# An mLSTM cell with a mixture-of-depths layer on one core: output gates loaded and outputs made some steps later, two batches' expert layers moved from step 8 to step 9

## The chip, the core and the metric

The kernel runs on one NeuronCore of a Trainium2 chip. The core has five engines that run beside each other, each with its own instruction queue in program order: TensorE (PE, matrix products and transposes into PSUM), VectorE (DVE), ScalarE (ACT), GpSimd (POOL) and SyncE (SP, which here only issues loads and the last store). Sixteen DMA engines move data between HBM and the on-chip memory; SP and POOL issue to them. The metric is device time in microseconds (us), the median over several executions. All data are float32.

## What is computed

There are 4 batches, 8 heads, 768 positions and a head width of 40. The recurrence over positions, then the expert layer over the rows of one batch:

```python
for t in range(S):
    m_new = np.maximum(f_gate[:, :, t] + m, i_gate[:, :, t])
    f_stab = np.exp(f_gate[:, :, t] + m - m_new)
    i_stab = np.exp(i_gate[:, :, t] - m_new)
    m = m_new
    C = f_stab[..., None, None] * C + i_stab[..., None, None] * np.einsum('bhd,bhe->bhde', vt, kt)
    n = f_stab[..., None] * n + i_stab[..., None] * kt
    h_tilde = np.einsum('bhde,bhe->bhd', C, qt)
    denom = np.maximum(np.abs(np.einsum('bhd,bhd->bh', n, qt)[:, :, None]), 1.0)
    o = 1.0 / (1.0 + np.exp(-o_gate[:, :, t]))
    y[:, :, t] = o * h_tilde / denom
# x[b, s] = the 8 heads of y side by side: 320 numbers
scores = np.einsum('bsd,d->bs', x, w_gate)
for b in range(B):
    top_idx = the 128 rows of x[b] with the highest scores
    ye = np.maximum(x[b, top_idx] @ w1, 0.0) @ w2          # 320 -> 1024 -> 320
    out[b] = x[b];  out[b, top_idx] += sigmoid(scores[b, top_idx])[:, None] * ye
```

## The kernel before

The sequence is cut into 12 steps n = 0 to 11 of 256 positions, three for each batch (batch b = n // 3). A step handles all 8 heads. The order of all work is written out by hand: every engine does its instructions in the order of the program text, and waits only for the data it needs and for buffers to come free.

**A step on TensorE** (lines 675 to 743): `scores(n)` multiplies k and q of the step; `turn(n + 1, "kT")` transposes the next step's k; `update(n + 1)` forms the next step's additions to the state C in the PSUM buffer pU, of which there is one; `read(n)` applies the states to q, `turn(n + 1, "qT")` transposes the next q, and `attend(n)` applies the masked scores to the weighted v. The second argument of turn is a number of `fill` products with no use of their own, which only keep TensorE going.

**The other engines in a step.** DVE: `masked(n)` applies the causal mask, `states(n + 1)` adds pU to the running states, `divide(n)` makes y. `router(i)` on DVE forms the scores of the rows of step i. ACT: copies out of PSUM (kT, qT), `widen`, and `sigmoid(n)`, which makes so from the output gates o. POOL: `weigh(n + 2)` weights v, `output(n)` makes x = y * so and `store(n)` sends it to the output. There are four buffers each of k, q, v, o and y, and three of so.

**The expert layer of a batch** needs the scores of its three steps. `spread(b, ...)` puts them side by side with TensorE transposes and an ACT copy; `ranks(b)` counts for each row how many scores are higher, half of it by DVE compares and half by ACT signs; `select(b)` makes a 0/1 matrix of the ranks; `numbers(b, ...)` turns that into row numbers (a small product on TensorE, then index arithmetic on DVE); `fetch(b)` gathers the 128 rows from the output with an indirect DMA issued by POOL; `fetched(b)` transposes them; `layer1`, `layer2` and `weighed` compute; `add(b)` is an indirect DMA from POOL that adds the result onto the output rows. `layers(n)`, lines 628 to 673, takes the place of the rest of step 8: it holds the layers of batches 0 and 1 and the selection of batch 2, and makes the outputs of steps 6, 7 and 8. Batch 2's layers run in step 11 and the tail, batch 3's in the tail.

**Loads.** Every load is issued by SP. `load(n)` is v, k and q of a step (320 KB each), `load_o(n)` its output gates (320 KB). Lines 100 to 107 issue the first ones, and the table `queue` (line 624) says in which step's program text the others stand. SP runs through that list in order and holds at an entry whose buffer is not yet free. Pieces of a load of k, v and o are rows of 40 floats.

## Time and profile before

| | us |
|---|---|
| median of 3 runs | 163.75 |
| lowest, highest | 161.92, 165.38 |
| the profiled execution, device time | 163.37 |
| its span, first to last instruction | 161.3 |

The granted clock of TensorE is 0.989 over the span. Time between the span and the device time, 2.07 us, lies around the instructions.

| Queue, kind | packets | MB | share of 16 engines |
|---|---|---|---|
| q1, hardware (loads by SP) | 89920 | 18.75 | 65.1% |
| q0, software (stores, fetches and adds by POOL) | 1728 | 4.92 | 11.0% |

How to read the rows that follow in the prediction. A row of the timeline is: start in us, duration in us, engine, line of the program, operation, output <- input, shape, count, and in brackets the idle time before it and what ended it. A row of the stages is: stretch in us, its length, then the busy time and the number of instructions of each engine, the granted clock of TensorE (1.00 is full speed), the share of the DMA engines and the GB/s that they moved. PEld is TensorE's loading of weights, which runs beside its products. An SPq row is SP issuing a DMA, not the transfer itself.

### The profile page before, as it was taken

The numbers are of one execution on the slowest core, as the hardware profiler recorded it, in microseconds if no ns is written. First come the engines' busy times: TensorE is split into PE (matmuls) and PEld (weight loads), VectorE is DVE, ScalarE is ACT, GpSimd is POOL, SyncE is SP. The second block draws the span as 40 slices with busy tenths as digits, with TensorE's granted clock in tenths as the row PEclk, the third lists the DMA queues.
The fourth block names the chain that finished last, engine by engine and source line by source line (L and its number), as shares of the span: only waits on it lengthen the run. The fifth ranks groups of instructions, "written<-read, shape, count | busy, mean of one in ns | idle before, by whom it ended". The sixth has DMA issues, their size and how long they took to land.

```text
span 161.3 us, 6676 instructions
## 1 busy us (share of the span) xinstructions
PE 144.5 (90%) x2864; PEld 125.4 (78%) x2864; DVE 95.2 (59%) x251; ACT 89.0 (55%) x179; POOL 84.5 (52%) x114
## 2 busy tenths in 40 slices
PE   7989899998998998899989989799999999999900
PEld 7779789997987987799878779579888897898500
DVE  6478384656769957594596542197776959411000
ACT  1667396566598747425475675874648669213000
POOL 7137278988575492892004969847480924212020
PEclk9999999999999999999999999999999999999995
DMA  4999899999979989999989999999513210330110
GB/s 88 198 163 196 137 169 205 188 186 205 194 169 227 187 161 208 175 262 296 157 240 232 206 266 172 216 190 184 100 45 87 46 39 4 81 41 0 53 51 2
DMA packets 91880, 24.31 MB, mean 151 GB/s; under 512 B 88097, under 2 KB 90466, under 8 KB 91842
## 3 DMA queue, kind: packets, MB, share of 16 engines
q1 hardware_dynamic: 89920, 18.75, 65.1%
q0 software_dynamic: 1728, 4.92, 11.0%
q8 instruction: 24, 0.39, 1.1%
q10 hardware_dynamic: 194, 0.13, 0.3%
q14 instruction: 14, 0.11, 0.2%
HBM read 19.20 MB, written 4.59 MB: 147 GB/s over the span
## 4 chain that ended last, share of the span: by engine, by line
PE 63%; DMA 14%; ACT 7%; issue 5%; DVE 5%; ACTq 1%; POOL 1%; DVEq 0%; POOLq 0%
PE pt L232 10%; DMA k<-in_k_dram 9%; PE pU L267 9%; PE py L576 8%; PE pH L332 7%; PE pH L322 6%; PE pU L560 6%; PE pS L300 4%; PE ph L560 2%; DMA i_sb<-in_i_gate_dram 2%; PE pU L564 2%; DMA xe<-out_dram,idx 2%; PE pX L498 2%; ACT sgn L423 1%; PE pt L221 1%
## 5 line engine op out<-in xcount | busy, mean ns | idle before, releaser
L244 POOL TENSOR_TENSOR wv<-v,cols 64x656 f32<-64x656 f32 x23 | 30.1, 1312 | 25.0 <-DMA v<-in_v_dram 14.1
L354 POOL TENSOR_TENSOR x<-y,so 128x320 f32<-128x320 f32 x24 | 21.1, 896 | 10.9 <-DVE y L346 4.2
L236 ACT COPY qT<-pt 128x512 f32<-128x512 f32 x24 | 13.8, 635 | 17.2 <-PE pt L232 17.2
L250 ACT ACTIVATE so<-o 64x320 f32<-64x320 f32 x48 | 22.4, 467 | 0.9
L234 ACT COPY kT<-pt 128x512 f32<-128x512 f32 x24 | 13.3, 587 | 15.0 <-PE pt L232 15.0
L369 DVE CUSTOM_DVE_ANT_0 scr<-x,wg 128x320 f32<-128x320 f32 x22 | 13.8, 628 | 8.1 <-POOL x L354 6.5
L576 PE MATMUL py<-w,hT 128*128 128x320 f32 x64 | 18.2, 437 | 0.3 <-ACT qT L236 0.3
L279 DVE TENSOR_TENSOR C<-pU,C 128x164 f32<-128x164 f32 x40 | 13.1, 327 | 7.0 <-PE pU L267 5.9
L267 PE MATMUL pU<-wv,k 128*64 128x82 f32 x384 | 16.5, 237 | 0.7 <-issue 0.7
L267 PEld LDWEIGHTS pU<-wv,k 128*64 128x64 f32 x384 | 14.5, 137 | 2.8 <-issue 2.2
L332 PE MATMUL pH<-wv,P 128*64 128x82 f32 x384 | 16.3, 237 | 0.0
L576 PEld LDWEIGHTS py<-w,hT 128*128 128x128 f32 x64 | 11.8, 190 | 5.1 <-ACT qT L236 0.5
L332 PEld LDWEIGHTS pH<-wv,P 128*64 128x64 f32 x384 | 14.4, 136 | 1.8 <-issue 1.0
L232 PE MATMUL pt<-ident,k 128*128 128x128 f32 x96 | 13.7, 279 | 2.3 <-DMA k<-in_k_dram 2.1
L361 POOL DMA_DIRECT2D out_dram<-x x22 | 13.9, 635 | 3.3 <-POOL x L354 3.3
L418 DVE TENSOR_SCALAR_CACHE_REDUCE cmp<-sb,x 128x768 f32<-128x768 f32 (+2 forms) x14 | 12.0, 857 | 6.0 <-ACT sb L412 5.7
L300 PE MATMUL pS<-qT,kT 40*64 40x64 f32 x768 | 14.8, 221 | 0.8 <-issue 0.5
L306 DVE TENSOR_TENSOR P<-pS,mask 128x1024 f32<-128x1024 f32 x12 | 14.6, 1214 | 0.6 <-PE pS L300 0.6
L523 POOL DMA_INDIRECT xe<-out_dram,idx x4 | 4.3, 1086 | 19.9 <-DVE den L341 13.8
L322 PE MATMUL pH<-C,qT 40*64 40x41 f32 x704 | 14.0, 229 | 0.8 <-issue 0.6
L300 PEld LDWEIGHTS pS<-qT,kT 40*64 40x64 f32 x768 | 12.8, 134 | 2.3 <-issue 0.7
L232 PE MATMUL pt<-ident,qw 128*128 128x128 f32 x96 | 13.1, 279 | 1.4 <-ACT qw L216 1.4
(141 smaller groups left out, 229.6 us busy)
## 6 DMA issues: line engine op xcount, KB each, us to landing
k<-in_k_dram SPq DMA_DIRECT2D x24, 160.0 KB, 5.0
q<-in_q_dram SPq DMA_DIRECT2D x12, 320.0 KB, 5.4
v<-in_v_dram SPq DMA_DIRECT2D x24, 160.0 KB, 4.8
o<-in_o_gate_dram SPq DMA_DIRECT2D x24, 160.0 KB, 5.0
out_dram<-x POOLq DMA_DIRECT2D x22, 160.0 KB, 4.4
w<-in_moe_w_dram SPq DMA_DIRECT2D x2, 640.0 KB, 5.8
w<-in_moe_w_dram SPq DMA_DIRECT2D x2, 512.0 KB, 6.0
out_dram<-x SPq DMA_DIRECT2D x2, 160.0 KB, 2.6
```

Source lines behind the costliest of these rows:

```text
L232: PE.transpose(pt[:, p, :], src[:, c, 2 * p:2 * p + 2, :].rearrange("s j d -> s (j d)"), ident)
L236: ACT.copy(out=T.rearrange("e p (u t) -> e t p u", t=2)[:, c], in_=pt)
L244: (DVE if n == 0 and r else POOL).tensor_tensor(out=wv_t[n % 3][o, :, :, r], in0=v_t[n % NB][o], op=OP.mult, in1=cols[s][o, 0:2, b * H:b * ...
L250: ACT.activation(out=so_t[n % 3][64 * c:64 * c + 64, r], in_=o_t[n % NO][64 * r:64 * r + 64, c], func=AF.Sigmoid)
L267: PE.matmul(pU[64 * j:64 * j + 64, c, p], k_t[n % NB][:, c, 2 * p + j, :], wv_t[n % 3][:, c, 2 * p + j], start=True, stop=True)
L300: PE.matmul(pS[o, j, c, p, :], kT[e, p, t], qT[e, p, t], start=True, stop=True)
L306: DVE.tensor_tensor(out=P.rearrange(flat), in0=pending[n].pop("pS").rearrange(flat), op=OP.mult, in1=mask.unsqueeze(1).to_broadcast([128, ...
L322: PE.matmul(g["pH"][64 * c:64 * c + 64, NP * j + p, r], g["qT"][e, p, t], state[n, 2 * c + r][e, p, :], start=(c, j) not in g["begun"], st ...
L332: PE.matmul(g["pH"][64 * c:64 * c + 64, NP * j + p], g["P"][:, j, c, p, :], wv_t[n % 3][:, c, 2 * p + j], start=(c, j) not in g["begun"], ...
L354: POOL.tensor_tensor(out=x.rearrange(order, j=2, d=D), in0=pending[n]["y"][:, r].rearrange("s (j p) d -> s j p d", j=2), in1=o.rearrange(o ...
L361: (POOL if n < N - 1 else SP).dma_start(out=out[b, a:a + 128, :].rearrange("(r t) d -> t r d", t=64), in_=x_t[b % 2][64 * c:64 * c + 64, 2 ...
L576: PE.matmul(d["py"], hT_t[:, f, half(b)], w2[:, f, :], start=(f == 0), stop=(f == NF - 1))
```

## The change

The loads of the output gates move back in SP's list, so that k, v and q of later steps stand ahead of them: o(0) behind load 2, o(1) behind load 3, and so on; loads 7, 8 and 9 move to earlier steps' text, the first-layer weights behind load 9. The outputs of steps 1 to 5 are made later, by the table `made` (step 7 makes 4 and 5), their scores by the table `scored`. Step 10 makes 10. `layers` now runs in step 9 and makes the outputs of 6, 7, 8 and 9. The spread of batch 0 moves from step 3 to step 4, its ranks, selection and numbers from step 4 to step 5. The spread of batch 1 moves from step 7 into `layers`, behind `read`, and into the buffer pU. `numbers(2)` and `fetch(2)` move from step 9 to step 10, and `add(1)` moves from the end of `layers` to behind `fetch(2)`, ahead of `output(10)`. The fills of step 2 go from 6 to 4 and those of step 5 from 4 to 2.

```diff
     wg = const.tile([128, DM], FP, name="wg")
+    load(2)
     load_o(0)
-    load(2)
-    load_o(1)
...
-        if pool is None:
+        if pool is ps_u:
+            pB = ps_u.tile([128, 2, 512], FP, name="pU")
+        elif pool is None:
...
-    queue = {0: (load, 3, load_o, 2), 1: (load, 4, load_o, 3, load, 5, load_o, 4), 2: (load, 6, load_o, 5),
-             4: (load, 7, load, 8, weights1, None, load_o, 6), 5: (load_o, 7, weights2, None, load_o, 8), 6: (load, 9),
-             7: (load, 10), 9: (load_o, 9, load_o, 10, load, 11, load_o, 11)}
+    queue = {0: (load, 3, load_o, 1), 1: (load, 4, load_o, 2, load, 5), 2: (load, 6, load_o, 3), 3: (load, 7),
+             4: (load, 8, load_o, 4, load_o, 5), 5: (load, 9, weights1, None, load_o, 6),
+             6: (load_o, 7, weights2, None), 8: (load_o, 8, load_o, 9, load, 10), 10: (load_o, 10, load, 11, load_o, 11)}
+    made = {0: (0,), 2: (1,), 3: (2,), 5: (3,), 7: (4, 5), 10: (10,)}
+    scored = {1: (0,), 3: (1,), 4: (2,), 6: (3,), 8: (4, 5), 10: (9,)}

     def layers(n):
         fetched(0)
         read(n)
+        dep[1] = {"sb": spread(1, 0, 2 * NS, ps_u)}
         ranks(1)
         select(1)
         attend(n)
         layer1(0, 0)
         numbers(1, ps_t.tile([128, 3], FP, name="pi", tag="t"))
         fetch(1)
-        sigmoid(n - 2)
+        sigmoid(6)
...
         turn(n + 1, "qT")
         dep[2] = {"sb": spread_copy(pB, 2 * NS)}
+        sigmoid(9)
+        output(9)
+        store(9)
         ranks(2)
         layer2(1)
         weighed(1)
         select(2)
         weigh(n + 2)
         update(n + 1)
         states(n + 1)
-        add(1)
...
-        if n == 8:
+        if n == 9:
             layers(n)
             continue
...
-        if n == 4:
+        if n == 5:
             ranks(0)
             select(0)
         if more:
-            turn(n + 1, "kT", (0, 2, 6, 2, 2, 4)[n] if n < 6 else 0)
+            turn(n + 1, "kT", (0, 2, 4, 2, 2, 2)[n] if n < 6 else 0)
             widen(n + 1)
         if 0 < n and more:
             update(n + 1)
-            if n != 9:
+            if n != 10:
                 states(n + 1)
-            if n not in (3, 6, 7, 9):
-                router(n - 1)
+            for i in scored.get(n, ()):
+                router(i)
...
         read(n)
-        if n == 9:
+        if n == 10:
             numbers(2, ps_s.tile([128, 2, 512], FP, name="pi", tag="s")[:, 0, 0:3])
             states(n + 1)
-        if n + 2 < N and n != 7:
+            fetch(2)
+            add(1)
+        if n < 8:
             weigh(n + 2)
...
-            if n in (3, 7):
-                dep[n // 4] = {"sb": spread(n // 4, 0, 2 * NS)}
-            if n not in (6, 7):
-                sigmoid(n)
+            if n == 4:
+                dep[0] = {"sb": spread(0, 0, 2 * NS)}
+            for i in made.get(n, ()):
+                sigmoid(i)
...
-        if n == 4:
+        if n == 5:
             numbers(0, spare(n + 1)[:, 1, 0:3])
-        if n == 9:
-            fetch(2)
-        if more and n not in (6, 7):
-            output(n)
-            store(n)
+        for i in made.get(n, ()):
+            output(i)
+            store(i)
```

More of the change, by code (lines that the diff above doesn't have):

```diff
@@ L637, in layers @@
         fetch(1)
-        sigmoid(n - 2)
-        output(n - 2)
-        store(n - 2)
+        sigmoid(6)
+        output(6)
+        store(6)
         layer1(0, 4)
@@ L643, in layers @@
         valued(0)
-        sigmoid(n - 1)
-        output(n - 1)
-        store(n - 1)
+        sigmoid(7)
+        output(7)
+        store(7)
         layer2(0)
-        router(n - 2)
-        router(n - 1)
+        router(6)
+        router(7)
         fetched(1)
         weighed(0)
-        sigmoid(n)
-        output(n)
-        store(n)
+        sigmoid(8)
+        output(8)
+        store(8)
         valued(1)
         layer1(1, 0)
-        router(n)
+        router(8)
         layer1(1, 4)
@@ L688, in _fast @@
             states(0)
-        if n in (3, 6, 11):
+        if n == 11:
             router(n - 1)
-        if n == 4:
+        if n == 5:
             ranks(0)
@@ L698, in _fast @@
             update(n + 1)
-            if n != 9:
+            if n != 10:
                 states(n + 1)
-            if n not in (3, 6, 7, 9):
-                router(n - 1)
+            for i in scored.get(n, ()):
+                router(i)
         if not more:
@@ L719, in _fast @@
             turn(n + 1, "qT")
-            if n in (3, 7):
-                dep[n // 4] = {"sb": spread(n // 4, 0, 2 * NS)}
-            if n not in (6, 7):
-                sigmoid(n)
+            if n == 4:
+                dep[0] = {"sb": spread(0, 0, 2 * NS)}
+            for i in made.get(n, ()):
+                sigmoid(i)
         else:
@@ L731, in _fast @@
         divide(n)
-        if n == 4:
+        if n == 5:
             numbers(0, spare(n + 1)[:, 1, 0:3])
-        if n == 9:
-            fetch(2)
-        if more and n not in (6, 7):
-            output(n)
-            store(n)
+        for i in made.get(n, ()):
+            output(i)
+            store(i)
         if n == 0:
```

## The prediction

> **What bounds the kernel now.** I read the page first, then the stages (one row a step: a step starts where TensorE starts its scores), then single rows.
>
> ```profile
> PE 144.5 (90%) x2864; PEld 125.4 (78%) x2864; DVE 95.2 (59%) x251; ACT 89.0 (55%) x179; POOL 84.5 (52%) x114
> DMA  4999899999979989999989999999513210330110
> PE 63%; DMA 14%; ACT 7%; issue 5%; DVE 5%; ACTq 1%; POOL 1%; DVEq 0%; POOLq 0%
> ```
> ```profile
> core 0: us, PE busy (x) PEld busy (x) DVE busy (x) ACT busy (x) POOL busy (x), PEclk, DMA share, GB/s
> 20.96:28.71 7.75, 7.59 (x214) 6.81 (x213) 4.54 (x12) 6.05 (x12) 6.20 (x18) 1.00 0.93 189
> ...
> 62.70:70.80 8.10, 7.00 (x194) 6.11 (x192) 6.02 (x14) 4.37 (x8) 6.84 (x8) 1.00 0.93 180
> 70.80:78.24 7.44, 7.44 (x217) 6.78 (x214) 3.63 (x9) 3.54 (x6) 2.38 (x2) 1.00 1.07 288
> 78.24:108.84 30.60, 28.41 (x358) 23.18 (x355) 18.53 (x45) 20.24 (x44) 17.22 (x18) 1.00 1.02 209
> 108.84:115.76 6.92, 6.92 (x201) 6.28 (x199) 5.16 (x16) 3.30 (x7) 4.09 (x3) 1.00 1.11 167
> ...
> 123.16:161.30 38.14, 29.42 (x347) 24.92 (x344) 15.09 (x44) 13.62 (x36) 10.34 (x11) 0.95 0.15 34
> ```
> TensorE carries the chain (63%), yet until about slice 28 the DMA engines are as full. The rows are steps 1, 6, 7, 8 (with the layers), 9 and 11 with the tail. Step 7 is TensorE without a gap (7.44 of 7.44); step 6 lost 1.1 us. What else TensorE does in a step:
>
> ```profile
> 29.80 1.60 PE L221 MATMUL pt<-hot 128*128 128x128 f32 x12
> 65.58 0.63 PE L232 MATMUL pt<-ident,k 128*128 128x128 f32 x4 [0.44 <-DMA k<-in_k_dram]
> 76.20 0.82 PE L405 MATMUL pB<-ident,x 128*128 128x128 f32 x6
> 76.95 1.36 PE L332 MATMUL pH<-wv,P 128*64 128x82 f32 x32
> ...
> 85.86 0.31 PE L517 MATMUL pi<-place,sel 128*128 128x3 bf16 x6
> ```
> A spread takes 76.95 - 76.20 = 0.75, so a bare step is 7.44 - 0.75 = 6.69; a fill is 1.60/6 = 0.27; numbers() 0.3. Steps 1 to 7 hold seven bare steps, 16 fills, two spreads and one numbers: 46.8 + 4.3 + 1.5 + 0.3 = 52.9. They took 78.24 - 20.96 = 57.3. So 4.4 us were lost there, in the stage where the queue of loads sets the pace (the wait for k in the row at 65.58 is one such place). That is what the change can win, with four fills.
>
> **The loading stage after the change.** SP's queue runs in program order, so the place of a tile in it, not the step, decides when it comes.
>
> ```profile
> 22.23 1.72 SPq L65 DMA_DIRECT2D v<-in_v_dram  x2
> ...
> 58.88 3.47 SPq L65 DMA_DIRECT2D k<-in_k_dram  x2
> ...
> 63.17 2.77 SPq L65 DMA_DIRECT2D v<-in_v_dram  x2
> 66.47 1.34 SPq L65 DMA_DIRECT2D k<-in_k_dram  x2
> ```
> From v3 (22.23) to v8 (63.17) the queue issued 19 tiles of 320 KB: 40.9/19 = 2.15 us each, the stores beside them counted in. k7's issue ended at 62.35 and TensorE went on with it at 65.58: landing takes 3.2 us more. After the change o stands behind k, v and q: k4 and k5 have one o fewer ahead of them, k6 to k8 two. Up to k9 there are now 29 tiles of k, v, q and six of o; up to k8 before, 26 and six, issued by 67.81. So k9 is three tiles later: 67.8 + 6.5 = 74.3, less one or two stores that are put off (stores 4 and 5 now follow step 7; an estimate of at most 2.15 each): 71 to 73, landed 74.2 to 76.2. Without any loss step 8 begins at 20.96 + 7 x 6.69 + 12 x 0.27 + 0.75 + 0.3 = 72.1 (the spread of batch 0 and numbers(0) lie in steps 4 and 5), and its second half of k9 is wanted about 1.7 us on, at 73.8. So 0.4 to 2.4 are lost, and I take 1.4; k4 to k8 come out with 0 to 1 us to spare by the same count, so that this last one decides. Step 9 then begins at 72.1 + 6.7 + 1.4 = 80.2 (79.2 to 81.2). Waits for buffers do not hold the queue up: loads 7, 8 and 9 reuse tiles that were given up a step or more before their turn. Behind load 9 come q9 (2.15) and the first weights, 1.3 MB, by the 288 GB/s of step 7 4.5 us: issued by 78.7, landed by 82; layer1 wants them at 80.2 + 5 or so, the sum of what stands ahead of it in step 9. They would cost only if they were 3 us later.
>
> Behind step 9's start TensorE has to do what stood behind step 8's: the layers, 30.60, now with the spread of batch 1 in them, +0.75; a step like the old step 9, 6.92; step 11 with the tail, 38.14: together 76.4. At equal end, 161.3, step 9 would have to begin at 84.9. So the loads and fills bring 84.9 - 80.2 = 4.7 us, before any new wait. The moved output, sigmoid and router calls are the same in number and lie on ACT, POOL and DVE, which are half idle in the sum (55, 52 and 59%); their order makes three new waits:
>
> **First wait: spread(1) inside the layers.** Before, 9.7 us lay between the spread (76.20) and numbers(1) (85.86); now there are attend and half a layer.
>
> ```profile
> 77.06 0.80 ACT L412 COPY sb<-pB 128x768 f32<-128x768 f32 x1
> 80.94 1.00 DVE L418 TENSOR_SCALAR_CACHE_REDUCE cmp<-sb,x 128x768 f32<-128x768 f32 x1
> 84.18 0.96 DVE L472 TENSOR_TENSOR sel<-iota,cnt 128x768 bf16<-128x768 f32 x1
> 83.23 2.05 PE L560 MATMUL pU<-xeT,w 128*128 128x128 f32 x16
> ```
> Copy 0.8, then compares to the end of the selection 85.14 - 80.94 = 4.2: 5.0 us. Cover: attend 1.3 and layer1 85.86 - 83.23 = 2.6. That leaves 1.1 us. Outputs 4 and 5 stand behind each other on POOL in step 7, so that router(5), ahead of divide(8) on DVE, can make read(9) late by up to 1.5 more. I take 1.8 (1.1 to 2.6).
>
> **Second wait: sigmoid(9) ahead of ranks(2)'s signs on ACT.** Queued behind it are the signs, for which DVE's halving waits, then select(2) and states(10); update(11) waits for states(10), since both use the one pU buffer.
>
> ```profile
> 107.19 0.19 ACT L423 ACTIVATION_READ_ACCUMULATOR sgn<-sb,x 128x1 f32 x1
> 107.41 1.00 DVE L433 TENSOR_SCALAR cnt<-cnt 128x3 f32<-128x3 f32 x1
> 109.67 1.05 DVE L279 TENSOR_TENSOR C<-pU,C 128x164 f32<-128x164 f32 x3
> 110.95 1.35 PE L267 MATMUL pU<-wv,k 128*64 128x82 f32 x32
> 115.17 1.93 ACT L250 ACTIVATE so<-o 64x320 f32<-64x320 f32 x4
> 107.10 1.28 POOL L244 TENSOR_TENSOR wv<-v,cols 64x656 f32<-64x656 f32 x1 [1.57 <-DMA out_dram<-yg,idx]
> 51.42 0.16 DVE L433 TENSOR_SCALAR cnt<-cnt 128x3 f32<-128x3 f32 x1
> ```
> Signs end 107.38, halving begins 107.41; the last read of pU ends 110.72 and TensorE begins 110.95. The slack is 0.2, the sigmoids are 1.93: 1.7 us of new wait. The halving took 1.00 there against 0.16 at 51.42, and ended with POOL's weigh (108.38). If it is late and finds POOL idle, it costs 0.8 less; if it meets both halves of weigh(11), up to 0.9 more: 0.9 to 2.6, I take 1.7. [...]
>
> **Third wait: add(1) between fetch(2) and output(10) on POOL.** Before, add(1) ran in the layers. Now POOL's order in step 10 is fetch(2), add(1), output(10), and add(1) waits for fetch(2)'s rows to have landed. Behind it wait output(10), router(10) on DVE and the spread of batch 3 on TensorE.
>
> ```profile
> DMA to landing us min/median/max: 3.1/3.2/6.6
> ```
> ```profile
> 113.30 0.31 PE L517 MATMUL pi<-place,sel 128*128 128x3 bf16 x6
> 114.03 0.16 DVE L482 SCALAR_TENSOR_TENSOR idx<-pi,off 128x1 int32<-128x1 f32 x1
> 116.95 0.82 DVE L346 TENSOR_TENSOR y<-pH,rec 128x640 f32<-128x640 f32 x1
> 124.97 1.70 POOL L354 TENSOR_TENSOR x<-y,so 128x320 f32<-128x320 f32 x2 [3.74 <-DVE y L346]
> 127.73 0.32 PE L405 MATMUL pB<-ident,x 128*128 128x128 f32 x1 [0.32 <-DVE x L369]
> 139.93 1.70 POOL L589 DMA_INDIRECT out_dram<-yg,idx  x1 [4.00 <-ACT yg L585]
> ```
> From numbers(2): index 114.19 - 113.30 = 0.9, fetch landed 3.2, add(1) 1.7, and 0.5 as an estimate for two starts on POOL: 6.3. y is ready 4.5 after numbers(2) in the like step (116.95 + 0.82), 0.4 sooner if DVE's additions before it are not held up. So output(10) is 1.8 to 2.2 late, and the row at 127.73 shows no slack: TensorE waited there already. I take 2.1; the quickest rows give 1.0, and a landing of 4.2 with a slower add 3.7.
>
> **Sum.** 80.2 + 76.4 + 1.8 + 1.7 + 2.1 = 162.2, and 0.3, an estimate, for o(0), which stands three tiles (6.5 us) later in the queue and lands about when sigmoid(0) wants it: 162.5, against 161.3. The profiled execution took 163.37 with 2.07 around the span, so 164.6; the median shown, 163.75, is 0.2% above that execution.
>
> **Rivals.**
> Faster: the three waits stay at their low ends (1.1 + 0.9 + 1.0) and k9 is in time (step 9 at 78.8): 78.8 + 76.4 + 3.0 = 158.2, time 160.3. For it: DMA carried 288 GB/s in step 7, so the queue can run faster than 2.15 a tile. Against: three low ends at once. 0.14.
> Slower: add(1) blocks POOL for longer. If fetch(2) lands as the slowest did (6.6), output(10) is 3.4 us later than in my sum: 165.9, time 168.0. It decides from a landing of about 5.5 us on. Against it: the slow landing fell where the DMA engines were full, and step 10 is nearly free of loads. 0.18.
> The change does not do what it says: the loads keep 2.15 a tile and no put-off store frees room. k9 lands at 77.5, step 9 begins at 82.5: 164.8, time 166.9. For it: shares of 0.93 and more in each step of loading. 0.13.
> The clock falls during a wait.
>
> ```profile
> 153.00:155.00 2.00, 0.00 (x0) 0.00 (x0) 0.49 (x1) 0.00 (x0) 1.04 (x1) 1.00 0.06 16
> 155.00:157.00 2.00, 0.00 (x0) 0.00 (x0) 0.00 (x0) 0.00 (x0) 0.00 (x0) 1.00 0.25 86
> 157.00:161.30 4.30, 0.00 (x0) 0.00 (x0) 0.00 (x0) 0.00 (x0) 0.00 (x0) 0.60 0.01 2
> ```
> From 153.0 on there is no matmul; four us later the clock is still 1.00, then it falls. The third wait is 2 to 3.7 us, so it should not reach that. If it did, work of some 4 us at half clock would cost 2 to 4: time 166.6 to 168.6. [...] 0.03.
>
> **How the numbers follow.** The forecast case has 0.52: 164.6, by itself 162 to 167. The range 160.4 to 168.4 reaches to the faster and the slower rival. About 2% of 163.75 (3.3 us) is what a measurement can tell from no change. Faster by more than that (under 160.5): most of the faster rival, 0.13. Slower (over 167.0): the slower rival, half of the third, the clock and the forecast's own upper edge, 0.18 + 0.07 + 0.03 + 0.04 = 0.32. Within: 0.55.
>
> **What would show it.** In the changed kernel's profile: k waits gone in steps 3 to 6 and one left before k9; step 9 beginning near 80; gaps on TensorE before numbers(1), before update(11), and before the spread of batch 3, the last with POOL sitting idle between fetch(2) and add(1). If step 9 begins before 79 or the gaps sum to under 3.5 us, the kernel is faster and I was wrong; if it begins after 82, the loads were not hurried.

## The result, and the profile after

| | us |
|---|---|
| before, median of 4 runs | 164.15 |
| after, median of 4 runs (lowest, highest) | 180.29 (180.02, 181.26) |
| ratio, with its 95% interval | 1.108 (1.095 to 1.121) |
| the profiled execution, device time; its span | 180.50; 178.4 |

Here and below a median is over all runs of a kernel, a ratio with its interval is over its fast runs alone (those within 1.5% of its fastest), and the profiled executions of e11 and e12 are slow ones, so that their rows serve for places and not for sums.

The changed kernel is 11% slower; the forecast was 164.6, in a range up to 168.4. First the rows of the page that answer to those of before:

```profile
PE 150.2 (84%) x2856; PEld 131.2 (74%) x2856; DVE 95.8 (54%) x251; ACT 88.8 (50%) x179; POOL 87.0 (49%) x114
...
PEclk9999999999999999996599999997569969999995
DMA  4999989799899999999998973243941330220110
...
PE 11%; issue 10%; DMA 3%; POOL 3%; DVE 1%; ACT 0%; POOLq 0%; DVEq 0%
```
TensorE is busy 5.7 us longer with practically the same products. That is the granted clock, which fell in three places (slices 19 and 20, 28 to 30, 33). The DMA engines are slack from slice 25 on and have a lump again at slice 29. The chain of waits sums to 28%: followed back from the end, it stops inside the kernel. Its earliest piece is GpSimd's weighting of v, `weigh`, at 120.6. The stages, one row a step (steps 8, 9 with the layers, 10, 11 with the tail), columns as before:

```profile
75.83:87.28 11.45, 9.61 (x210) 8.57 (x208) 6.77 (x18) 6.27 (x12) 6.83 (x9) 0.75 1.03 256
87.28:119.50 32.22, 29.45 (x347) 24.13 (x345) 17.51 (x43) 21.87 (x47) 18.07 (x21) 0.98 0.65 142
119.50:136.02 16.52, 9.30 (x216) 8.04 (x214) 6.68 (x19) 4.15 (x10) 3.80 (x3) 0.69 0.60 96
136.02:178.40 42.38, 31.09 (x347) 26.29 (x344) 13.62 (x44) 13.61 (x36) 12.77 (x13) 0.90 0.18 38
```
Against the forecast's terms: step 9 begins at 87.28, forecast 80.2 + 0.3, so 6.8 late. The layers took 32.22, forecast 30.60 + 0.75 + 1.8 = 33.15, so 0.9 less. Step 10 took 16.52, forecast 6.92 + 1.7 = 8.6: 7.9 more. The rest took 42.38, forecast 38.14 + 2.1 = 40.2: 2.1 more. Together 15.9, the whole distance from 162.5 to 178.4.

Step 10, in the timeline (start, duration, engine, line, operation; SPq rows are the queue of loads):

```profile
119.50 1.16 PE L299 MATMUL pS<-qT,kT 40*64 40x64 f32 x64
127.87 2.14 PE L231 MATMUL pt<-ident,k 128*128 128x128 f32 x8 [7.22 <-DMA k<-in_k_dram]
...
122.73 0.99 SPq L65 DMA_DIRECT2D v<-in_v_dram  x2
123.82 1.52 SPq L65 DMA_DIRECT2D k<-in_k_dram  x2
...
119.20 3.50 POOL L243 TENSOR_TENSOR wv<-v,cols 64x656 f32<-64x656 f32 x2
```
and what the queue of loads waited for (total, times, longest):

```profile
SPq L65 <- POOL wv L243: 21.6, 1, 21.6
```
The queue stood still for 21.6 us, until 122.7, waiting for GpSimd's `weigh` that ends at 122.70. Behind it k of step 11 came late, and TensorE stood idle for 7.2 us. The program text gives the reason. `layers(9)` runs in step 9 and calls `weigh(11)`; the table puts `load(11)` into step 10's text. v of step 11 goes into the buffer of v of step 7, so in program order `weigh(11)` is a reader of that buffer that comes before the load, and the load waits for it. (In the changed kernel step 11 thereby weighs the v of step 7.) The clock, in stretches of 2 us:

```profile
122.00:124.00 2.00, 0.00 (x0) 0.00 (x0) 1.90 (x5) 0.00 (x0) 0.70 (x1) 0.62 0.07 11
...
128.00:130.00 2.00, 2.00 (x10) 1.33 (x11) 0.00 (x0) 0.59 (x1) 0.00 (x0) 0.50 1.32 224
...
132.00:134.00 2.00, 2.00 (x79) 1.77 (x78) 0.09 (x1) 0.00 (x0) 0.00 (x0) 0.82 0.00 0
...
142.00:144.00 2.00, 0.88 (x3) 0.59 (x4) 1.82 (x5) 0.00 (x0) 1.70 (x3) 0.74 0.31 50
```
TensorE's last product of step 10's scores ends at 120.66; the clock is at half from about 122.5 to 132.7, so the first products after the wait run at half speed: the 8 transposes at 127.87 take 2.14, in the same step of the kernel before 1.09. The same happens behind the shorter wait of 2.80 at 140 to 143, where the clock is at half from 143.0 to 146.4.

### The profile page after: what moved, and what is told of

It reads as the page before. It is cut to its first block, busy times and chain, and to the rows that moved or that the text cites. A ratio compares the mean times of both kernels' runs of the same rounds, so it can differ in the third digit from the quotient of the medians.

```text
span 178.4 us, 6653 instructions
## 1 busy us (share of the span) xinstructions
PE 150.2 (84%) x2856; PEld 131.2 (74%) x2856; DVE 95.8 (54%) x251; ACT 88.8 (50%) x179; POOL 87.0 (49%) x114
## 5 line engine op out<-in xcount | busy, mean ns | idle before, releaser
L243 POOL TENSOR_TENSOR wv<-v,cols 64x656 f32<-64x656 f32 x23 | 32.6, 1419 | 24.0 <-DMA v<-in_v_dram 15.4
L233 ACT COPY kT<-pt 128x512 f32<-128x512 f32 x24 | 13.0, 588 | 21.6 <-PE pt L231 21.5
L368 DVE CUSTOM_DVE_ANT_0 scr<-x,wg 128x320 f32<-128x320 f32 x22 | 14.9, 677 | 8.7 <-POOL x L353 7.0
L266 PE MATMUL pU<-wv,k 128*64 128x82 f32 x384 | 17.6, 246 | 1.4 <-issue 0.7
L266 PEld LDWEIGHTS pU<-wv,k 128*64 128x64 f32 x384 | 15.5, 144 | 3.8 <-issue 3.2
L331 PE MATMUL pH<-wv,P 128*64 128x82 f32 x384 | 17.4, 246 | 0.0
L231 PEld LDWEIGHTS pt<-ident,k 128*128 128x128 f32 x96 | 11.2, 148 | 8.2 <-issue 7.7
L331 PEld LDWEIGHTS pH<-wv,P 128*64 128x64 f32 x384 | 15.4, 144 | 2.1 <-issue 1.3
L321 PE MATMUL pH<-C,qT 40*64 40x41 f32 x704 | 14.8, 236 | 1.8 <-issue 1.8
L321 PEld LDWEIGHTS pH<-C,qT 40*64 40x64 f32 x704 | 13.2, 141 | 3.4 <-issue 2.7
L231 PE MATMUL pt<-ident,qw 128*128 128x128 f32 x96 | 13.9, 291 | 1.4 <-ACT qw L215 1.4
```

The costliest lines, as they stand in the source:

```text
L231: PE.transpose(pt[:, p, :], src[:, c, 2 * p:2 * p + 2, :].rearrange("s j d -> s (j d)"), ident)
L243: (DVE if n == 0 and r else POOL).tensor_tensor(out=wv_t[n % 3][o, :, :, r], in0=v_t[n % NB][o], op=OP.mult, in1=cols[s][o, 0:2, b * H:b * ...
L266: PE.matmul(pU[64 * j:64 * j + 64, c, p], k_t[n % NB][:, c, 2 * p + j, :], wv_t[n % 3][:, c, 2 * p + j], start=True, stop=True)
L321: PE.matmul(g["pH"][64 * c:64 * c + 64, NP * j + p, r], g["qT"][e, p, t], state[n, 2 * c + r][e, p, :], start=(c, j) not in g["begun"], st ...
L331: PE.matmul(g["pH"][64 * c:64 * c + 64, NP * j + p], g["P"][:, j, c, p, :], wv_t[n % 3][:, c, 2 * p + j], start=(c, j) not in g["begun"], ...
L368: DVE.tensor_tensor_reduce(out=scr, in0=x[:, r, 0:DM], in1=wg, scale=1.0, scalar=0.0, op0=OP.mult, op1=OP.add, accum_out=x[:, r, DM:DM + 1])
```

## The experiments

All times below stand beside runs of the kernel before on the same chip; ratios are against those runs.

| run | median us | ratio (95%) | step 1 to step 9, us |
|---|---|---|---|
| before | 163.9 to 165.2 | 1 | 57.28 + 6.92 = 64.2 |
| after | 180.29 | 1.108 (1.095 to 1.121) | 87.28 - 20.82 = 66.5 |
| e1 load(11) | 172.10 | 1.050 (1.042 to 1.057) | 85.47 - 21.20 = 64.3 |
| e2 and add(1) | 168.01 | 1.020 (1.010 to 1.031) | 87.04 - 22.97 = 64.1 |
| e3 and sigmoid(9) | 166.28 | 1.013 (1.004 to 1.022) | 86.10 - 20.48 = 65.6 |
| e4 e1 and fills | 170.83 | 1.042 (1.033 to 1.052) | 87.07 - 21.16 = 65.9 |
| e5 e3 and numbers(0) | 165.61 | 1.009 (1.005 to 1.014) | 85.89 - 21.30 = 64.6 |
| e6 e5 and spread(0) | 167.19 | 1.023 (1.011 to 1.034) | 85.15 - 21.24 = 63.9 |
| e7 e3, old places of o, o(5) in step 2 | 184.03 | 1.125 (1.117 to 1.132) | see there |
| e8 e3, old places of o | 168.92 | 1.028 (1.019 to 1.036) | 86.31 - 20.92 = 65.4 |
| e9 e5 and output(2) | 167.44 | 1.018 (1.010 to 1.026) | 86.76 - 20.62 = 66.1 |
| e10 e9 and router(4), (5) | 166.83 | 1.009 (1.003 to 1.014) | 85.03 - 21.30 = 63.7 |
| e11 e3, one o | 167.98 | 1.021 (1.011 to 1.031) | see there |
| e12 before, one o | 166.30 | 1.011 (1.001 to 1.021) | see there |
| e13 e3, small weights | 165.16 | 1.010 (1.006 to 1.013) | 85.49 - 21.07 = 64.4 |
| e14 e3, one o, small weights | 163.17 | 1.000 (0.996 to 1.003) | 82.66 - 20.77 = 61.9 |

The last column runs from the start of step 1 to the start of step 9 in the profiled execution; for the kernel before, whose layers stand in step 8, it is steps 1 to 7 and its plain step 9. The forecast had 59.2 there (80.2 less 20.96).

**Load(11) ahead of its reader (e1).**

```diff
-             ..., 8: (load_o, 8, load_o, 9, load, 10), 10: (load_o, 10, load, 11, load_o, 11)}
+             ..., 8: (load_o, 8, load_o, 9, load, 10), 9: (load, 11), 10: (load_o, 10, load_o, 11)}
```

> The changed kernel with load(11) moved from step 10's text to step 9's, ahead of weigh(11), so that v of step 11 is what weigh(11) reads again. Theory A: the 7.2 us wait for k11 in step 10, and the half clock behind it, come from the place of load(11) behind weigh(11) in program order (SP holds at v11 until GpSimd has read the old tile at 122.7). Then k11 lands before 110, the wait is gone, step 10 is about 8.6 us long (6.9 of work and the 1.7 that update(11) waits for states(10)) instead of 16.5: span about 170.5, time about 172.6. Rival B: k11 is late because the queue of loads is long or the DMA engines are full there; then k11 still comes after 120 and the time falls by under 3 us, to 177 or more. Rival C: the clock stays low for a reason other than the wait; then step 10 still runs 3 us at half clock and the time is about 175.

172.10, span 169.9. Step 10 of e1, as a stage and in the timeline:

```profile
118.83:127.17 8.34, 7.00 (x217) 6.32 (x215) 6.67 (x19) 4.04 (x10) 3.80 (x3) 1.00 0.15 33
```
```profile
122.35 1.36 PE L266 MATMUL pU<-wv,k 128*64 128x82 f32 x32 [1.34 <-DVE C L278]
...
119.20 0.69 DVE L434 TENSOR_SCALAR cnt<-cnt 128x3 f32<-128x3 f32 x1 [1.85 <-ACT sgn L424]
...
104.72 2.32 SPq L65 DMA_DIRECT2D k<-in_k_dram  x2
```
k of step 11 is issued 19 us earlier, its wait and the half clock are gone, and step 10 is 8.2 us shorter. Theory A holds. What remains in the step is the wait of update(11) that the prediction had named second: VectorE's halving (the row at 119.20) waits 1.85 for the signs on ACT. In the kernel after it lay hidden behind the k wait.

**Add(1) behind output(10) (e2), sigmoid(9) behind the signs (e3), fills in the wait (e4).**

```diff
             fetch(2)
-            add(1)
...
             store(i)
+        if n == 10:
+            add(1)
```

> The kernel before in this call with add(1) moved in step 10 behind output(10) and store(10). Theory A: the 2.8 us wait of the spread of batch 3 comes from add(1) standing ahead of output(10) on GpSimd, and it alone lets the clock fall from 143 to 146. Then the wait falls to about 0.3, no half clock follows, and the span is 2.6 and 1.2 to 1.7 shorter than with load(11) moved alone: about 166.5, time about 168.6. Rival B: output(10) waits for something else (y of step 10, or store(9)); then the wait keeps over 1.5 us and the gain is under 1.5. Rival C: add(1) moved back is late for a later instruction (store(10), add(2), the fetch of batch 3); then the gain at the spread is lost again in the tail, and the time stays above 171.

e3 builds on e2, as e2 does on e1; e4 builds on e1.

```diff
         dep[2] = {"sb": spread_copy(pB, 2 * NS)}
-        sigmoid(9)
-        output(9)
-        store(9)
         ranks(2)
         layer2(1)
         weighed(1)
+        sigmoid(9)
         select(2)
         weigh(n + 2)
+        output(9)
+        store(9)
```

> In addition sigmoid(9) stands behind weighed(1), and output(9) and store(9) behind weigh(11). Theory A: sigmoid(9) ahead of the signs of ranks(2) makes update(11) wait 1.7 us for states(10). Then signs end about 1.9 us earlier relative to step 9's start, update(11) starts without a wait of over 0.3, and the span is 1.7 shorter than that of the kernel with load(11) and add(1) moved: about 165, time about 167. Rival B: the halving on VectorE waits for GpSimd's weigh(11) and not for the signs; then the wait stays over 1 us and the gain is under 0.7. Rival C: output(9) after weigh(11) makes router(9) late on VectorE in step 10; then the wait moves to divide(10) and the gain is under 0.7.

```diff
-            fetched(b - 1, 2)
+            fetched(b - 1, 14)
```

> The kernel with load(11) moved, and 12 more fills (3.2 us of TensorE by 0.27 each) ahead of the transposes of batch 2's rows in step 11, in the place where TensorE waits 2.8 us for the spread of batch 3. Theory A: the clock falls because TensorE stood idle for 2.8 us. Then the fills lie in the wait, it ends at the same time or up to 0.4 later, the clock stays 1.00 behind it, and the span is 0.8 to 1.4 shorter than with load(11) moved alone. Rival B: the half clock behind the wait does not come from the idle time; then it stays and the span is the same to 0.5 longer. Rival C: the fills displace work that would otherwise run ahead of the wait; then the span is 1 to 3 longer.

The wait for the spread of batch 3 and the layer behind it, in the timelines of e1, e2 and e4:

```profile
134.13 0.32 PE L406 MATMUL pB<-ident,x 128*128 128x128 f32 x1 [2.84 <-DVE x L368]
...
134.94 3.34 PE L561 MATMUL pU<-xeT,w 128*128 128x128 f32 x16
```
```profile
132.48 0.32 PE L406 MATMUL pB<-ident,x 128*128 128x128 f32 x1 [0.32 <-DVE x L368]
```
```profile
130.63 3.39 PE L220 MATMUL pX<-hot 128*128 128x128 f32 x28
...
135.58 1.95 PE L561 MATMUL pU<-xeT,w 128*128 128x128 f32 x16
```
With add(1) behind output(10) the wait is back at the 0.32 of the kernel before; 168.01, a gain of 4.1, is more than the 2.5 of the wait: step 11 with the tail took 42.7 in e1 (169.9 - 127.17) and 38.1 in e2 (166.0 - 127.94), and most of the rest is the half clock. The fills show that part alone (41.2 in e4, 169.0 - 127.76): the spread comes no earlier, but TensorE was busy meanwhile, and the 16 products of layer1 take 1.95 instead of 3.34. The times of e1 and e4 (172.10 and 170.83) have overlapping intervals; the verdict rests on the rows. e3 (166.28; 1.7 less than e2 by the medians, with overlapping intervals) takes the wait of update(11) away: step 10 went from 8.36 in e2 to this row of e3:

```profile
119.02:125.95 6.93, 6.93 (x216) 6.29 (x214) 5.63 (x18) 4.53 (x10) 3.81 (x5) 1.00 0.24 52
```
With these three repairs, e3 still isn't below the kernel before. What is missing is the gain of the loads: the last column of the table stands at 64 to 66, whatever was repaired.

**The selection of batch 0 (e5, e6).** In step 5 TensorE waits 1.2 to 2.0 us at numbers(0) in after and e1 to e4. VectorE in the kernel after, step 5 (timeline), and the row of TensorE that waits:

```profile
59.03 0.96 DVE L473 TENSOR_TENSOR sel<-iota,cnt 128x768 bf16<-128x768 f32 x1
59.91 0.32 DVE L282 COPY C<-pU 128x164 f32<-128x164 f32 x1
60.27 1.05 DVE L278 TENSOR_TENSOR C<-pU,C 128x164 f32<-128x164 f32 x3
...
61.38 0.29 PE L518 MATMUL pU<-place,sel 128*128 128x3 bf16 x6 [1.18 <-DVE C L278]
```
The selection itself is ready at 59.99. But numbers(0) writes into the buffer pU of the next step's update, and waits until states(6), 0.32 + 1.05, has read it. In the kernel before it stood in step 4, behind the shorter states(5), and had no such wait. In e1, e2, e3 and e4 (waits of 1.40 to 1.97) step 6 then ran at a clock of 0.79 to 0.80. e5 moves numbers(0) behind read(6), into another buffer; e6 also moves the spread:

```diff
-        if n == 5:
-            numbers(0, spare(n + 1)[:, 1, 0:3])
...
         read(n)
+        if n == 6:
+            numbers(0, ps_s.tile([128, 2, 512], FP, name="pi", tag="s")[:, 0, 0:3])
```

> The kernel with load(11), add(1) and sigmoid(9) moved, and numbers(0) taken from the end of step 5 to step 6, behind read(6), into a buffer of its own (pi instead of pU). Theory A: the 1.9 us wait in step 5 comes from numbers(0) standing behind the compares of ranks(0) and the additions of states(6) on VectorE, and the 1.5 us that step 6 loses at half clock come from that wait. Then both go, update(7) does not wait for the index either, and the span is 2.5 to 3.4 shorter than that of the kernel without this edit: about 161, time about 163. Rival B: the loads set the pace of steps 5 to 8; then waits for k of 2 us or more in sum take the place, and the gain is under 1.2. Rival C: fetch(0), later now, makes layer 1 in step 9 wait; then a wait of over 0.5 for xe stands at the start of step 9.

```diff
-            if n == 4:
-                dep[0] = {"sb": spread(0, 0, 2 * NS)}
...
         attend(n)
+        if n == 4:
+            dep[0] = {"sb": spread(0, 0, 2 * NS)}
         divide(n)
```

> In addition the spread of batch 0 stands behind attend(4) instead of ahead of it. Theory A: in its old place it waits for router(2) on VectorE (0.4 to 1.2 us in four profiles, none in the fifth, where k was late); then step 4 is 0.4 to 1 shorter and the span 0 to 1 shorter than with numbers(0) moved alone: time about 162.5. Rival B: the copy behind the spread, later now, makes ranks(0) late on VectorE in step 5; then step 5 is longer by what step 4 gains, and the time is the same within 0.4.

e5: 165.61, a gain of 0.7 where theory A had 2.5 to 3.4; rival B's size, but not its reason, since no k wait came. Steps 5 and 6 of e5, and two waits of its timeline:

```profile
55.67:62.95 7.28, 7.28 (x215) 6.64 (x213) 6.95 (x14) 5.91 (x13) 2.57 (x2) 1.00 0.92 167
62.95:71.50 8.55, 7.51 (x201) 6.57 (x199) 7.92 (x26) 4.25 (x8) 5.73 (x6) 1.00 0.96 186
```
```profile
54.13 0.32 PE L406 MATMUL pB<-ident,x 128*128 128x128 f32 x1 [1.18 <-DVE x L368]
...
71.50 1.19 PE L299 MATMUL pS<-qT,kT 40*64 40x64 f32 x64 [0.56 <-DVE den L340]
```
Step 5 lost its wait and step 6 its low clock, but VectorE has the same work to do and is late a step further on, and in this execution step 4 waited longer for the spread. In e6 that wait is gone, but the scores of step 5 waited 0.89 for the copy of the spread, and its 167.19 is slower by the medians, with overlapping intervals: read(9) waited 1.96 for y of step 8, and the clock fell behind it (the layers took 34.60, in e5 32.49).

**The places of o (e7, e8).** To see what the order of the loads is worth, o(0) to o(6) went back next to k, v and q.

```diff
+    load_o(0)
     load(2)
-    load_o(0)
+    load_o(1)
...
-    queue = {0: (load, 3, load_o, 1), 1: (load, 4, load_o, 2, load, 5), 2: (load, 6, load_o, 3), 3: (load, 7),
-             4: (load, 8, load_o, 4, load_o, 5), 5: (load, 9, weights1, None, load_o, 6),
+    queue = {0: (load, 3, load_o, 2), 1: (load, 4, load_o, 3, load, 5, load_o, 4), 2: (load, 6, load_o, 5), 3: (load, 7),
+             4: (load, 8, load_o, 6), 5: (load, 9, weights1, None),
```

> The kernel with load(11), add(1) and sigmoid(9) moved, with the output gates o(0) to o(6) put forward again in the list of loads, to the places next to k, v and q that they have in the kernel before; everything else of the change stays. Theory A: the new order of the loads is worth its 2.15 us for each tile of o that k does not wait behind; then waits for k of 1.5 us or more in sum return in steps 3 to 6, and the span is 1.5 to 4 longer than without this edit: time 168 to 170. Rival B: steps 1 to 6 are held by VectorE and by the clock, and what the loads gain is lost there; then k waits return in part but in the cover of the others, and the time is the same within 1 us: 165.5 to 167.5.

184.03: the experiment fell into the same trap as the change. o(5) stood in step 2's text ahead of sigmoid(1), whose buffer it takes; step 1's output then waited for the gates of step 5 and used them. Step 3's transposes in e7:

```profile
61.68 1.97 PE L232 MATMUL pt<-ident,qw 128*128 128x128 f32 x8 [18.74 <-ACT qw L216]
```
e8 has o(5) at the same place of the list, in step 3's text:

```diff
-             2: (load, 6, load_o, 5), 3: (load, 7),
+             2: (load, 6), 3: (load_o, 5, load, 7),
```

> The kernel with load(11), add(1) and sigmoid(9) moved, and o(0) to o(6) put forward again to the places next to k, v and q that they have in the kernel before; o(5) stands at the same place of the list as there, but behind sigmoid(1) in program order, so that no tile is written ahead of its reader. Theory A: the new order of the loads is worth its 2.15 us for each tile of o that k does not wait behind; then waits for k of 1.5 us or more in sum return in steps 2 to 6 and the time is 1.5 to 4 above that of the kernel without this edit: 168 to 170. Rival B: steps 1 to 6 are held by VectorE and by the clock behind its waits, and what the order of the loads wins is lost there again; then the k waits return in the cover of the others and the time is the same within 1 us: 165.3 to 167.3.

168.92, in theory A's range. But the intervals of e8 and e3 overlap, and the profile doesn't carry it: k waits came back (0.78 + 0.68 + 0.26 = 1.7), yet step 1 to step 9 took 65.4, in e3 65.6. In the profiled executions e8's span is 1.7 longer; 0.9 of it stands in the layers (33.85, in e3 32.92), at this wait of read(9), with a low clock behind it:

```profile
89.81 1.13 PE L322 MATMUL pH<-C,qT 40*64 40x41 f32 x48 [1.44 <-DVE y L346]
```
So in the stage of loads itself rival B holds; whether the order of the loads is worth anything in the total stays open.

**Earlier x for the spread, routers behind divide(8) (e9, e10).**

```diff
-    made = {0: (0,), 2: (1,), 3: (2,), 5: (3,), 7: (4, 5), 10: (10,)}
+    made = {0: (0,), 2: (1,), 5: (3,), 7: (4, 5), 10: (10,)}
...
             widen(n + 1)
+            if n == 3:
+                sigmoid(2)
...
+        if n == 3:
+            output(2)
+            store(2)
         if n < 8:
             weigh(n + 2)
```

> The kernel with load(11), add(1), sigmoid(9) and numbers(0) moved, and step 3's sigmoid(2) put ahead of update(4), its output(2) and store(2) ahead of weigh(5). Theory A: in step 4 the spread of batch 0 waits 0.4 to 1.2 us because router(2) is late on VectorE: its x comes late from GpSimd, and its two products take 1.3 to 1.8 while GpSimd weighs, against 0.5 when GpSimd rests. Then with x 3 us earlier the wait falls to under 0.3, step 4 to about 8.5 from 9.9, and the span is 1 to 1.5 shorter than with numbers(0) moved: time about 164.3. Rival B: router(2) is late because of its place behind states(5) on VectorE; then the wait stays, and weigh(5), later now, adds 0.3 or more. Rival C: the next k or the states wait in its place; then the gain is under 0.5.

```diff
-    scored = {1: (0,), 3: (1,), 4: (2,), 6: (3,), 8: (4, 5), 10: (9,)}
+    scored = {1: (0,), 3: (1,), 4: (2,), 6: (3,), 10: (9,)}
...
         divide(n)
+        if n == 8:
+            router(4)
+            router(5)
```

> In addition router(4) and router(5) stand behind divide(8). Theory A: ahead of divide(8) they make y of step 8, and so read(9), 0.5 to 2 us late (0.46, 0.53 and 1.96 in three profiles). Then the wait of read(9) is gone and the span is 0.5 shorter than without this edit: time about 163.8. Rival B: the selection of batch 1, which starts with the spread behind read(9), then waits for router(5), and numbers(1) in the layers gets the 0.5 as a wait instead; then the time is the same within 0.3.

Both missed. In e9 and e10 the wait of the spread is gone, and the weighted v is late in its place (rival C of e9): 0.85 in e9 and 1.61 in e10. The wait of read(9) that e10 was to remove isn't in e9 either, so e10 can't test its theory A; numbers(1) waited 0.77 in it. e10's 63.7 is among the shortest of that column, yet not 1 us below the kernel before.

**Without the loads of o, without the weights (e11 to e14).** These runs ask how long the stage takes when the loads are few.

```diff
     def load_o(n):
+        if n > 0:
+            return
...
-    in_=o_t[n % NO][64 * r:64 * r + 64, c]
+    in_=o_t[0][64 * r:64 * r + 64, c]
```

> The kernel with load(11), add(1) and sigmoid(9) moved, without the loads of o(1) to o(11): every step's output uses the gates of step 0. Up to k9 the queue then has five tiles fewer (10.7 us by 2.15 each), so k, v and q come as early as their buffers allow. Question: what holds steps 1 to 8 at 64 to 66 us in every variant, against 57.8 of bare work. Theory A, the loads: then no wait for k or v is left, and with steps that start evenly VectorE and GpSimd are in time too: steps 1 to 8 take under 61.5, time about 162 or less. Rival B, the order of the work on VectorE and GpSimd and the clock behind those waits: then numbers(0) in step 5 still waits over 1.2, step 6 still has a low clock, and steps 1 to 8 take over 63.5: time over 164.5.

> The kernel before, without the loads of o(1) to o(11): every step's output uses the gates of step 0. Up to k9 eight tiles fewer stand in the queue. Theory A, the loads alone cost the 4.4 us that steps 1 to 7 lost: then they take under 54.5 instead of 57.3, the k waits (1.8 in sum) are gone, and the time is 3 or more lower, 161 or less. Rival B: only the k waits go, other waits take their place, and steps 1 to 7 take 56 or more: the time falls by under 1.5.

Theory A of both runs fell: with eleven tiles of 320 KB less to load, neither kernel became faster (1.021 against e3's 1.013; 1.011 for the kernel before). Rival B's times held, but not its reason: in e11 numbers(0) waited 0.92 and step 6 ran at full clock. Where TensorE waited in e12, and then in the kernel after:

```profile
58.06 0.64 SPq L617 DMA_DIRECT2D w<-in_moe_w_dram  x1
...
71.82 0.88 PE L324 MATMUL pH<-C,qT 40*64 40x41 f32 x19 [3.09 <-issue]
```
```profile
73.80 0.94 SPq L616 DMA_DIRECT2D w<-in_moe_w_dram  x1
...
81.55 1.52 PE L321 MATMUL pH<-C,qT 40*64 40x41 f32 x47 [1.84 <-issue]
```
No tile and no engine releases these waits. The one of 1.84 is the wait in step 8 of the kernel after, behind which the clock is at half from about 81.5 on; step 8 takes 11.45. In these rows they begin 6 and 11 us behind the first load of the expert weights, wherever that stands. e13 and e14 load a seventh of the weights, without and with the cut of o:

```diff
-        for h in range(2):
-            f, g = slice(512 * h, 512 * h + 512), slice(2 * h, 2 * h + 2)
-            SP.dma_start(out=w1[:, :, f], in_=w1_in[0:256, f].rearrange("(j p) f -> p j f", j=2))
+        SP.dma_start(out=w1[:, :, 0:128], in_=w1_in[0:256, 0:128].rearrange("(j p) f -> p j f", j=2))
...
-                PE.matmul(ph[:, f // 2, f % 2, :], w1[:, j, (f0 + f) * 128:(f0 + f) * 128 + 128], xeT[:, j, :],
+                PE.matmul(ph[:, f // 2, f % 2, :], w1[:, j, 0:128], xeT[:, j, :],
```

> The kernel with load(11), add(1) and sigmoid(9) moved, with a seventh of the expert weights loaded: every block of 128 hidden columns uses the weights of the first block (0.36 MB instead of 2.6). The products keep their shapes and number. Theory A: TensorE's idle time put down to issue in steps 8 and 9 (1.8 us with load(11), add(1) and sigmoid(9) moved) comes from instruction blocks that arrive late behind the transfers of the weights; then it falls below 0.6 there, and the span is 1 to 2 shorter: time about 164.8. Rival B: the idle time is bound to places in the program and not to the weights; then it stays above 1.2 in steps 8 and 9, and the time is within 0.7 of 166.3.

> In addition no loads of o(1) to o(11): every step's output uses the gates of step 0. Up to the end of step 8 only k, v and q are loaded. Theory A: what the loads of o gave back was taken by late instruction blocks; with the weights gone too, the gain appears: steps 1 to 8 take under 63, time about 163 or less. Rival B: the order of work on VectorE and GpSimd holds the steps (numbers(0) behind the compares of ranks(0) and the additions of states(6), a spread behind router(2)), and its waits and the clock behind them stay: steps 1 to 8 take over 64 with fewer than 1 us of idle time put down to issue, and the time is above 164.5. Rival C: k, v and q alone fill the DMA engines up to k9; then waits for k or v of over 1 us in sum stand in steps 3 to 6.

In steps 8 and 9 of e3 the issue waits were 0.20 + 0.94 + 0.82 = 2.0; in e13 none of 0.15 or more is left there, in e14 one of 0.16. That fits theory A but doesn't show it: with all the weights the same sum goes from 0 in e4 over 0.4 in e5, e6 and e8 to 3.0 in e9, so two profiles without these waits can be chance. e13's gain by the medians is 1.1, with overlapping intervals; part went into a new wait, here with the two engines' rows ahead of it (timeline of e13), and, for comparison, the same product in e14:

```profile
83.27 2.11 POOL L353 TENSOR_TENSOR x<-y,so 128x320 f32<-128x320 f32 x2
83.52 1.15 DVE L368 CUSTOM_DVE_ANT_0 scr<-x,wg 128x320 f32<-128x320 f32 x1
...
88.62 1.13 PE L321 MATMUL pH<-C,qT 40*64 40x41 f32 x48 [1.49 <-DVE y L345]
```
```profile
80.84 0.48 DVE L370 CUSTOM_DVE_ANT_0 scr<-x,wg 128x320 f32<-128x320 f32 x1
```
The scores of a row block take 1.15 beside GpSimd's output and 0.48 without; four of them stand ahead of divide(8), and y of step 8 is late. e14 has the numbers of theory A: step 1 to step 9 takes 61.9, 3.7 less than in e3, and the time is 163.17. Between it and e11, which differs in the weights alone, lie 4.8 us of median (3.5 by the ratios), and the intervals are apart: with one o, the loads of the weights do cost time. Through which waits is not shown. Of the 3.7 us, 1.0 lies in step 5 (9.50 and 8.50) and 1.3 in step 6, here e3 and then e14:

```profile
63.38:71.73 8.35, 8.35 (x195) 7.55 (x193) 6.14 (x19) 3.07 (x5) 6.37 (x7) 0.80 1.04 209
```
```profile
61.27:68.34 7.07, 6.85 (x196) 6.17 (x193) 5.83 (x19) 3.08 (x6) 5.96 (x7) 1.00 1.09 229
```
There numbers(0) waited 1.93 in e3, with the low clock behind it, and 0.93 in e14. Both steps end before e3 issues its first load of weights (76.21), and step 8, behind that, is as long in both (7.58 and 7.54). Even so e14 only equals the kernel before.

## Why the prediction was wrong

**Failed: "Waits for buffers do not hold the queue up".** That step looked at loads 7, 8 and 9 alone. Load 11 holds the queue for 21.6 us. Of the 15.9 us between forecast and span, 7.9 are this step (e1: step 10 from 16.52 to 8.34). What it takes to see it was there, since the change moves `layers`, and with it `weigh(11)`, ahead of the text that loads v of step 11. I compared places in the list of loads and not, buffer by buffer, the load with the reader of the old tile.

**Failed: "So the loads and fills bring 84.9 - 80.2 = 4.7 us".** The loads came as forecast: k of step 9 was issued by 72.8 (forecast 71 to 73), and no wait for k of 0.15 or more is left in steps 1 to 8 of the kernel after. So the prediction's own sign, that step 9 after 82 means that the loads were not hurried, pointed the wrong way. The gain was sized from 4.4 us "lost" in steps 1 to 7, all put down to the queue of loads. These rows of the kernel before, with the 0.44 at 65.58, are all its waits for k there:

```profile
39.81 0.63 PE L232 MATMUL pt<-ident,k 128*128 128x128 f32 x4 [0.39 <-DMA k<-in_k_dram]
57.47 0.63 PE L232 MATMUL pt<-ident,k 128*128 128x128 f32 x4 [0.27 <-DMA k<-in_k_dram]
64.52 0.63 PE L232 MATMUL pt<-ident,k 128*128 128x128 f32 x4 [0.66 <-DMA k<-in_k_dram]
```
They sum to 1.8. All idle time of TensorE in these steps is 2.7 (busy 54.5 of 57.28), and the other 1.6 is product time that the count of bare steps (52.9) left out. The step also took it that nothing stands next behind the k waits. Next behind them were waits of the selection of batch 0 (numbers(0) behind states(6): 1.18 to 1.97, where my count had the 0.3 of its products; the spread behind router(2): up to 1.18), a wait that nothing releases (1.84 in step 8), and the clock behind either. The rival that the loads keep 2.15 a tile, 166.9, went that way, but had a third of the size (step 9 2.3 late instead of 6.8) and another reason.

**Right: the three new waits.** First, numbers(1) in the layers: 1.8 forecast, 1.35 in the kernel after (0.3 in e1 and e3, where a wait put down to issue just ahead took its place). Second, update(11) behind the signs: 1.7 forecast, 1.34 and 1.35 in e1 and e2, none in e3, where the halving no longer waits for the signs, so its cause is shown. Third, add(1) ahead of output(10): 2.1 forecast, 2.80 + 0.17 - 0.32 = 2.65 after, 0.32 in e2.

**Mis-sized: the clock.** It had 0.03 and was thought to need 4 us of idleness, from the rows at 153 to 157. That those rows show 1.00 is true, but they are one case, and the last section shows why it misleads. The fall behind the third wait was worth about 1.3 (e4 against e1, by the medians), the one in step 8 more: 2.6, if the 11.45 of step 8 is set against the 1.84 of the wait and the 7.0 of busy time that e1 to e4 show there; the clock was low there from 81.5 to 88.4, twice as long as behind the third wait. The clock did fall behind waits, as this rival had it, but behind shorter ones than it took: 2.80 in the kernel after, 1.21 in e2.

With load(11) in its place the change would have been a case of 172.1, still above the range; with all three waits repaired 166.3. No variant was shown to be below the kernel before.

## What to carry to other kernels

When a change moves a consumer and a load by hand in static buffers, write down for each buffer the order of load, reader and next load in program text: a load behind the wrong reader can cost a wait as long as the distance (here 21.6 us in the queue of loads and 7.22 on TensorE), and it shows in the trace as the load queue waiting for an engine. Removing the wait that comes last in a stage brings only the distance to the next one, so list for each step what would be ready second, and on which engine. Ask of each new wait of more than about 1.2 us, the shortest with a fall here (1.21 in e2), what TensorE has to do behind it, because it may be done at half clock; in e4 independent products in the wait brought that back (the 16 products behind it took 1.95 us, in e1 3.34).

## What the runs showed of the hardware

**The clock fell earlier than the rows of before showed, and on a grid of 3.41 us.** Behind waits of TensorE between 1.40 and 1.97 us it fell in some cases (such as 1.40 in e4 and 1.96 in e6) and stayed at 1.00 in others (1.47 in e13, 1.61 in e10, 1.86 in e9). The shortest wait with a fall behind it is this one of e2 in step 0; the same 27 products take 1.21 at full clock in the kernel before:

```profile
17.91 2.00 PE L266 MATMUL pU<-wv,k 128*64 128x82 f32 x27 [1.21 <-issue]
```
Behind 2.80 and 7.22 (the kernel after) and 2.84 (e1) it fell. Behind the 2.84 of e1 it was low for 3.4 us (0.81, 0.50, 0.84 in the stretches of 2 us from 134 on: 0.76 + 2.0 + 0.64):

```profile
134.00:136.00 2.00, 1.54 (x9) 1.36 (x10) 1.61 (x6) 0.58 (x1) 1.98 (x3) 0.81 0.41 83
136.00:138.00 2.00, 2.00 (x11) 1.98 (x10) 0.00 (x0) 0.00 (x0) 1.32 (x2) 0.50 0.31 82
138.00:140.00 2.00, 2.00 (x36) 1.67 (x36) 0.00 (x0) 0.80 (x3) 0.00 (x0) 0.84 0.00 0
```
Read in stretches of 0.1 us, the falls of one profile lie whole multiples of 3.41 us apart: in the kernel after they begin at 81.5, 122.5 and 143.0 (12 and 6 times 3.41) and last 6.83, 10.24 and 3.41, in e1 at 63.6 and 135.2 (21 times), in e2 at 18.1 and 65.9 (14 times). So it mattered here how a wait lay on that grid. From 10 us on, in all 16 profiles, a piece at full clock in which TensorE was idle for 1.68 us or more was each time followed by one at half clock, a piece with up to 1.18 never; in between both came. In the kernel after the pieces ahead of the three falls had 1.82, 1.83 and 2.80 idle, and the most of any other piece at full clock there, from 10 us to the last product, was 1.33. The 1.86 of e9 and the 1.47 of e13 lie across an edge (0.94 + 0.92 and 0.75 + 0.72), and the clock stayed. In the kernel before the products end at 152.9, inside a piece that ends at 154.4 with 1.5 idle; the next one is all idle, and the clock falls at its end, 157.9. That is why the 4 us of the prediction's rows show 1.00.

**Waits that nothing releases, 128 and 126 products apart in two profiles.** In the kernel before, 27 + 8 + 32 + 61 = 128 products lie between the issue waits that end at 17.50 (0.67) and 22.26 (0.16). In e9, from the first to the second of these rows there are 48 + 8 + 32 + 40 = 128 products, from the second to the third 24 + 3 + 48 + 6 + 32 + 13 = 126 (the rows between them are not shown):

```profile
83.60 0.91 PE L321 MATMUL pH<-C,qT 40*64 40x41 f32 x48 [0.70 <-issue]
88.04 0.58 PE L299 MATMUL pS<-qT,kT 40*64 40x64 f32 x24 [0.47 <-issue]
95.75 0.49 PE L561 MATMUL pU<-xeT,w 128*128 128x128 f32 x3 [1.86 <-issue]
```
```profile
q8 instruction: 24, 0.39, 1.0%
```
The instruction queue moves packets of 0.39 MB / 24 = 16 KB. The trace counts a product and its weight load as two instructions (2856 of each in the kernel after), so 128 products are 256 of them. Single waits of this kind took 1.84 (after), 1.86 (e9) and 3.09 (e12). That such a wait is a packet of instructions arriving late is an estimate of the author's from the places and the packets, and no run shows it. That the loads of the weights make it late is not shown either: e4 has all the weights and no such wait of 0.15 or more in steps 8 and 9, and in e2 one of 1.21 stands in step 0, before any weights are loaded.
